# One super-step of a fused attention and MLP kernel, its order of loads, splits, merges and inversions written anew

## Chip, cores and metric

The kernel runs on one core of a Trainium2 chip. The metric is the device time of one execution in microseconds (us). Five engines matter here: PE (TensorE, with its weight loads shown as PEld), DVE (VectorE), ACT (ScalarE), POOL (GpSimd) and SP (SyncE), whose queue starts nearly all DMA transfers. Each engine works through its own instructions in order.

## What is computed

A delta-rule attention over 768 steps for 4 batches of 8 heads (head dimension 48) gives 3072 tokens of width 384, and two MLPs follow.

```python
for t in range(S):
    y[:, :, t] = einsum('bhd,bhde->bhe', q[:, :, t], state)
    v_old = einsum('bhde,bhd->bhe', state, kt)
    state = state + bt * einsum('bhd,bhe->bhde', kt, vt - v_old)   # kt: key / its norm
...
h = maximum(x @ w_in, 0.0); x = h * h @ w_out                      # d_ff 2048
g = x @ w_gate; out = silu(g) * (x @ w_val) @ w_out                # d_ff 1536
```

## The kernel before

**Tiles and stages.** The sequence is cut into six super-steps J of 128 steps, and each into two chunks c of 64 steps. A chunk's recurrence is solved with the inverse of a triangular 64x64 matrix per head: a Gram matrix of the keys (`gram`, `gram0`), its mask and scaling, the inverse of its 32x32 diagonal blocks, merges that join blocks (`m1`, `m2`), and then `ks` (old state times keys), `u`, `y` (output) and `ku` (state update). For J >= 1 the blocks go through DRAM: `mout` writes the matrices to `m_scr`, `tload` reads the diagonal blocks of all heads into the one tile `T`, `inv` eliminates 30 rows on POOL, `nout` writes `T` to `n_scr`, and `nback` and `mback` read them into `NT`. `t11` then transposes on DVE what `m1` multiplies. For J = 0 the diagonal blocks are inverted on DVE at once for both chunks (`inv0`, as 16x16 halves); `dout` transposes the result into the tiles `ND` and `NDT`, `d1` and `d2` are the merges of the halves (64 tiny matmuls a chunk each, counted twice in the trace since fp32 takes two passes), and `dcopy` copies the result.

**The first MLP** runs under the attention of the next super-step: 16 blocks m of 128 hidden units. `moe1_h` is x @ w_in of block m (one group of six matmul passes, lines 915 or 947), `moe1_o` its part of the output (line 989). In super-step 0 the first six blocks are done in two halves of 256 tokens. The weights come in 16 pieces (pc, kd) of 768 KB (kd 0: w_in, kd 1: w_out). Each is loaded by `load_w1`, decoded from 64-bit words by an ACT operation (line 157) and three DVE steps (lines 162, 164, 169; `conv`, and `ahead` for the ACT part alone), and later split into a high and a low part for the fast matmul format: `high` on ACT (line 184) and `low` on DVE (line 187). Super-step 0 multiplies by the decoded weights themselves, all but its last two blocks; from super-step 1 on the split parts are used. The pool of weight tiles is full, so a piece's split form takes the tile of the piece that was split before it. `split_x` splits the tokens of the next super-step.

**Order.** PE and SP follow the order of the program text. In super-step 0 so do DVE, ACT and POOL. Ahead of the first `moe1_h` stands a startup written out by hand. After it, `slot` is called twice for each block of the MLP, once after the next `moe1_h` and once after the `moe1_o`, and it adds to a clock: 0.5 for a half block and 1 for a whole one, so that super-step 0 has 32 units and whole block m has the slots 2m and 2m + 1. The table `first` says at which clock value a stage of the attention or a load is issued, `conv_slot` keeps decoding at 1.8 steps a unit, and `split_slot` splits pieces at a rate from a start value. The pieces that are not split when the last `moe1_h` of super-step 0 has been issued are split there, one behind the other:

```python
if J < NJ - 1 and nxt[0] == J and nxt[3] == NM1 - 1:
    if nxt[1] == 0:
        while split1:
            split_one()
        lows_out()
        split_x(J + 1, 0, HT)
```

At the end of super-step 0 the three accumulators are copied to two tiles `ye`, which a DMA on POOL's queue stores (line 1006); they share their buffers, so the second waits for the store of the first.

Of the kernel before, what the change touches and what calls it, by code (L numbers as in the profile page):

```python
# [21 lines left out]
def delta_attention_moe_moe2_kernel(  # L22
# [46 lines left out]
    TOK = 128 * B  # L69
    HT = TOK // 2  # L70
    HMS = [6, 2, 1, 1, 1, 1]
    LAGS = [0, 0, 4, 0, 0, 0]
    NC = S // 64

    const = ctx.enter_context(tc.tile_pool(name="const", bufs=1))
# [137 lines left out]
    def load_w1(pc, kd):  # L213
        if (pc, kd) == FIRST:
            raw = xp.tile([128, 2 * PIECE], I32, tag="xh", name="raw")
        else:
            raw = wp.tile([128, 2 * PIECE], I32, tag="w", name="raw")
        load_piece((w_in, w_out)[kd], pc, kd == 1, raw)
        loaded[pc, kd] = raw
# [253 lines left out]

    def d_out():
        nc.vector.transpose(out=ND.rearrange("s x t -> s t x"), in_=T)
        nc.vector.transpose(out=NDT.rearrange("t x s -> t s x"), in_=TT)

    def d_rest():

# [632 lines left out]
    def conv(n):  # L1112

        conv_to(converted() + n)
# [7 lines left out]
    def merge16(w, c):  # L1122
        run_all((w, c, p) for p in P2)
# [20 lines left out]
    load_w1(0, 1)  # L1144
    run(("v", 0, 1))
    load_w1(1, 0)
    nc.gpsimd.memset(mask, 0.0)
    for b0 in (0, 64):
        nc.gpsimd.affine_select(
# [28 lines left out]
    run(("drest",))  # L1178
    run(("vn", 0, 0))
    run(("dout",))  # L1180
    merge16("d1", 0)
    run(("sq", 1, 1, 1))
    run(("root", 1, None, 0))
    run(("root", 1, None, 1))
    stage("mmask", 1, 0)
    stage("mmask", 1, 1)
    conv(1)
    merge16("d2", 0)
    ahead()
    run(("t11", 0, 0))  # L1190
    run(("dcopy", 0))
    stage("mbeta", 1, 0)
    stage("mout", 1, 0)
    run(("m1", 0, 0))
    conv(2)
    ahead()
    run(("m2", 0, 0))
    stage("mbeta", 1, 1)
    stage("mout", 1, 1)
# [2 lines left out]
    conv(2)  # L1202
    run(("u", 0, 0))
    held.clear()
    conv(1)
    ahead()
    stage("y", 0, 0)
    run_all(("tload", 1, c) for c in P2)
    run(("v", 1, 0))
    run(("mback", 1, 0))  # L1210
    run(("ku", 0, 0))
    merge16("d1", 1)
    run(("vn", 0, 1))
    run(("inv", 1, 0, 1, nc.gpsimd))
    conv(3)
    load_w1(1, 1)
    load_w1(2, 0)
    run(("loadq", 1, 0))
    load_w1(2, 1)
    run(("loadk", 2, 0))  # L1220
    PRE = converted()
    startup.clear()

# [10 lines left out]
    if True:  # L1234

        LOW2 = 300
        CR = 0.6
        RATE = 0.8
        SPLIT0 = 14
        SPLIT = 0.7  # L1240
        seq = []
        for J in range(NJ):
            seq += [(J, c0, HT, m) for c0 in (0, HT) for m in range(HMS[J])]
            seq += [(J, 0, TOK, m) for m in range(HMS[J], NM1)]
        first = {
            0: [("d2", 1, 0), ("d2", 1, 1)],
            0.5: [("ks", 0, 1)],
            1: [("t11", 0, 1), ("m1", 0, 1), ("dcopy", 1)],
            2: [("m2", 0, 1), ("loadw", 3, 0)],
            3: [("u", 0, 1)],  # L1250
            4: [("y", 0, 1, 0), ("y", 0, 1, 1), ("loadw", 3, 1), ("loadq", 1, 1)],
            5: [("ku", 0, 1), ("loadk", 2, 1), ("mback", 1, 1), ("v", 1, 1)],
            6.5: [("loadw", 4, 0)],
            7: [("amm", 1, 0), ("acopy", 0)],
            8: [("sq", 2, 0, 0), ("loadw", 4, 1)],
            9: [("sq", 2, 0, 1), ("sq", 2, 1, 0)],
            9.5: [("loadw", 5, 0)],
            10: [("sq", 2, 1, 1), ("root", 2, None, 0)],
            11: [("root", 2, None, 1), ("loadw", 5, 1)],
            12: [("amm", 1, 1), ("acopy", 1)],  # L1260
            12.5: [("loadw", 6, 0)],
            13: [("gram", 2, 0)],
            14: [("loadw", 6, 1)],
            15: [("gram", 2, 1)],
            15.5: [("loadw", 7, 0)],
            16: [("vn", 1, 0), ("asel", 0), ("vn", 1, 1), ("asel", 1)],
            16.5: [("nout", 1), ("nback", 1, 0), ("tload", 2, 0), ("tload", 2, 1), ("nback", 1, 1)],
            17: [("inv", 2, 0, 1, nc.gpsimd)],
            17.5: [("loadw", 7, 1)],
            18: [("ks", 1, 0), ("t11", 1, 0)],  # L1270
            19: [("m1", 1, 0)],
            20: [("m2", 1, 0)],
            21: [("u", 1, 0), ("v", 2, 0), ("mback", 2, 0)],
            22: [("t11", 1, 1), ("y", 1, 0, 0), ("y", 1, 0, 1), ("loadq", 2, 0)],
            23: [("ku", 1, 0), ("loadk", 3, 0), ("fetch", 1, 0, HT)],
            24: [("m1", 1, 1)],
            25: [("ks", 1, 1)],
            26: [("m2", 1, 1)],
            28: [("u", 1, 1), ("v", 2, 1), ("mback", 2, 1), ("vn", 2, 0)],
            29: [("y", 1, 1, 0), ("y", 1, 1, 1), ("loadq", 2, 1)],  # L1280
            30: [("ku", 1, 1), ("fetch", 1, HT, HT), ("loadk", 3, 1)],
            31: [("nout", 2), ("nback", 2, 0), ("vn", 2, 1)],
            34: [("agram", 2, 0)],
        }
        timed = [(i, name) for i, names in first.items() for name in names]
        for C in range(2, NJ):
            lag = LAGS[C]
            timed += [(2 * NM1 * (C - 1) + lag + i - 3, s) for i, slot_ in enumerate(plan(C, C + 1)) for s in slot_]
        timed.sort(key=lambda s: s[0])
        clock = [0.0]  # L1290

        def slot(J, n_, m):
            while timed and timed[0][0] <= clock[0] + 1e-6:
                run(timed.pop(0)[1])
            clock[0] += n_ / TOK
            if J == 0:
                conv_slot(PRE + int(STEPS * CR * clock[0]))
            if J == 0:
                split_slot(J, m, SPLIT * (clock[0] - SPLIT0))

        def split_slot(J, m, n):
            lows_out()
            if split1 and NCONV - len(split1) < n and 2 * split1[0][0] + 1 < m:
                split_one()

        moe1_h(*seq[0])
        moe1_low()
        for n, it in enumerate(seq):
            J, c0, n_, m = it
            if n and J and not seq[n - 1][0]:  # L1310
                order.close()
                order.enter_context(tc.manual_schedule(engines={mybir.EngineType.DVE, mybir.EngineType.Activation}))
            nxt = seq[n + 1] if n + 1 < len(seq) else None
            if nxt:
                moe1_h(*nxt)
                if J and nxt == (J, 0, HT, HMS[J] - 1):
                    split_x(J, HT, HT)
# [6 lines that stand above are left out]
                    if nxt[1] + nxt[2] == TOK and HMS[J + 1] < 2:  # L1324
                        split_x(J + 1, HT, HT)
            else:
                moe2_g(0, 0, pool2)
            slot(J, n_, m)
            moe1_low()
            moe1_o(*it, pool2)  # L1330
            slot(J, n_, m)
            if n + 1 < len(seq) and J == NJ - 1 and pool2 is None and not xraw and not timed:
                order.close()
                att.__exit__(None, None, None)
                held.append(1)
                pool2 = ctx.enter_context(tc.tile_pool(name="p2", bufs=4))
                conv2 = [(pc, kd) for pc in range(NM2 // 2) for kd in range(3)]
                raws2 = [(pc, kd) for pc in range(NM2 // 2) for kd in range(3)]
                n_end = n
                for _ in range(3):  # L1340
                    load_w2(*raws2.pop(0), pool2)
            if J == NJ - 1 and m == NM1 - 4:
                load_x2(0, pool2)
            if J == NJ - 1 and m == NM1 - 2:
                split_x2(0)
            if pool2 is not None:

# [73 lines left out]
```

## Time and profile before

| | us |
|---|---|
| median of 3 runs | 1094.08 |
| lowest, highest of the runs | 1094.03, 1294.63 |
| profiled execution, device time | 1093.18 |
| its span (first to last instruction) | 1091.5 |
| PE busy | 1011.7 (93%) |
| DVE, ACT, POOL busy | 575.3, 402.7, 232.4 |

The profiled execution agrees with the median to 0.1%. Its device time is 1.7 us longer than its span. A busy PE is not yet a fast PE: the granted clock has two levels, 1.0 (2.4 GHz) and 0.5 (1.2 GHz), and a stretch's mean lies between them.

### The profile page before, as it was taken

Reading aid. Unit: us, or ns where it says so; the run is one execution under the profiler, and the core shown is the slowest. Engines: PE = TensorE matmul, PEld = TensorE weight load, DVE = VectorE, ACT = ScalarE, POOL = GpSimd, SP = SyncE. Lnnn points to the kernel's source line nnn. Section 1 sums busy time; section 2 is a strip of 40 time slices with the busy share of each in tenths; the row PEclk is TensorE's granted clock in tenths of the full one; section 3 lists DMA queues with packets and bytes.
Section 4 is the critical chain, followed back from the end, with each engine's and each line's share of the span. In section 5 each row is a group of like instructions: output and inputs, shape, how many; then the busy total and the mean of one; then the engine's idle time right before and its main releaser. Section 6 shows DMA issues by size and latency. Waiting matters only on the chain.

```text
span 1091.5 us, 24143 instructions
## 1 busy us (share of the span) xinstructions
PE 1011.7 (93%) x10454; PEld 812.7 (74%) x10454; DVE 575.3 (53%) x940; ACT 402.7 (37%) x756; POOL 232.4 (21%) x365
## 2 busy tenths in 40 slices
PE   4368989579999999999999999999999999999998
PEld 4357635467777788788787878888888888888886
DVE  7627674447767757645536996343343343433333
ACT  7324644424344344333336874222222222222222
POOL 3584229210860850770000000000000000000000
PEclk9979988789999999999999999999999999999999
DMA  9272463143353352331114661010010010100000
GB/s 274 57 215 69 165 164 96 40 123 64 97 153 77 88 132 70 83 96 38 31 30 155 194 223 66 1 58 1 1 58 1 25 34 1 59 1 0 29 1 29
DMA packets 118249, 84.49 MB, mean 77 GB/s; under 512 B 91648, under 2 KB 95616, under 8 KB 118144
## 3 DMA queue, kind: packets, MB, share of 16 engines
q1 hardware_dynamic: 116944, 77.97, 25.8%
q0 software_dynamic: 1056, 4.72, 1.1%
q8 instruction: 82, 1.34, 0.5%
q10 hardware_dynamic: 144, 0.26, 0.1%
q14 instruction: 23, 0.19, 0.1%
HBM read 61.70 MB, written 21.23 MB: 76 GB/s over the span
## 4 chain that ended last, share of the span: by engine, by line
PE 73%; issue 10%; DVE 7%; DMA 5%; ACT 4%; SPq 1%; POOL 0%; DVEq 0%; ACTq 0%; POOLq 0%
PE ps_o L1084 13%; PE ps_g L1059 13%; PE ps_v L1059 13%; PE ps_y L989 12%; PE ps_h L947 10%; PE ps_h L915 3%; DMA y_scr<-ye 1%; PE ps_y L753 1%; DMA raw<-in_moe_w_gate_dram 1%; PE ps_g L401 1%; PE ps_u L716 1%; DVE w L187 1%; PE ps_k L701 1%; PE ps_a L525 1%; PE ps_s L737 1%
## 5 line engine op out<-in xcount | busy, mean ns | idle before, releaser
L947 PE MATMUL ps_h<-xh,w 128*128 128x512 f32 (+1 forms) x540 | 170.6, 376 | 0.0
L989 PE MATMUL ps_y<-hh,w 128*128 128x512 f32 (+1 forms) x528 | 133.3, 387 | 15.9 <-ACT ye L1005 6.9
L1059 PE MATMUL ps_g<-x2h,w 128*128 128x512 f32 x432 | 144.8, 389 | 0.0
L1059 PE MATMUL ps_v<-x2h,w 128*128 128x512 f32 x432 | 144.7, 389 | 0.0
L1063 DVE SCALAR_TENSOR_TENSOR th<-th,ps_g 128x512 f32<-128x512 f32 x72 | 49.5, 688 | 170.8 <-ACT th L1062 170.7
L574 POOL TENSOR_TENSOR TMP<-T 128x30 f32<-128x30 f32 (+9 forms) x150 | 89.3, 595 | 157.3 <-DMA T<-m_scr 145.9
L989 PEld LDWEIGHTS ps_y<-hh,w 128*128 128x128 f32 x528 | 94.2, 191 | 34.6 <-ACT ye L1005 7.1
L950 ACT ACTIVATE r<-ps_h 128x512 f32<-128x512 f32 (+1 forms) x90 | 49.4, 549 | 181.6 <-PE ps_h L947 181.6
L947 PEld LDWEIGHTS ps_h<-xh,w 128*128 128x128 f32 x540 | 99.8, 191 | 18.1
L1084 PE MATMUL ps_o<-ph,w 128*128 128x512 f32 x432 | 111.9, 389 | 1.5 <-ACT ye L1005 1.5
L1062 ACT ACTIVATE th<-ps_g 128x512 f32<-128x512 f32 x72 | 43.0, 598 | 180.0 <-PE ps_g L1059 179.9
L947 PE MATMUL ps_h<-xl,w 128*128 128x512 f32 (+1 forms) x270 | 99.7, 369 | 0.0
L1084 PEld LDWEIGHTS ps_o<-ph,w 128*128 128x128 f32 x432 | 81.0, 188 | 18.7 <-ACT ye L1005 1.9
L1066 ACT ACTIVATE ph<-th 128x512 fp32r<-128x512 f32 x72 | 45.5, 632 | 133.2 <-DVE th L1064 133.2
L1059 PEld LDWEIGHTS ps_g<-x2h,w 128*128 128x128 f32 x432 | 81.1, 188 | 17.2 <-ACT hh L951 0.4
L1059 PEld LDWEIGHTS ps_v<-x2h,w 128*128 128x128 f32 x432 | 81.1, 188 | 16.9
L581 POOL TENSOR_TENSOR T<-T,TMP 128x30 f32<-128x30 f32 (+9 forms) x150 | 91.2, 608 | 11.3
L1059 PE MATMUL ps_g<-x2l,w 128*128 128x512 f32 x216 | 84.0, 389 | 0.0
L1059 PE MATMUL ps_v<-x2l,w 128*128 128x512 f32 x216 | 84.0, 389 | 0.0
L966 DVE TENSOR_TENSOR r<-r 128x512 f32<-128x512 f32 (+1 forms) x73 | 49.2, 675 | 64.1 <-ACT hh L951 63.8
L989 PE MATMUL ps_y<-hl,w 128*128 128x512 f32 (+1 forms) x264 | 72.0, 382 | 3.5 <-DVE hl L967 3.5
L1064 DVE SCALAR_TENSOR_TENSOR th<-th,ps_v 128x512 f32<-128x512 f32 x72 | 49.5, 688 | 44.8 <-PE ps_v L1059 44.7
(139 smaller groups left out, 1495.5 us busy)
## 6 DMA issues: line engine op xcount, KB each, us to landing
raw<-in_moe_w_out_dram SPq DMA_DIRECT2D x14, 768.0 KB, 5.4
raw<-in_moe_w_in_dram SPq DMA_DIRECT2D x8, 768.0 KB, 10.3
KT<-in_kt_dram SPq DMA_DIRECT2D x12, 448.0 KB, 5.3
m_scr<-M SPq DMA_DIRECT2D x20, 256.0 KB, 2.5
KB<-in_kn_dram SPq DMA_DIRECT2D x12, 384.0 KB, 5.2
AQ<-in_q_dram SPq DMA_DIRECT2D x24, 192.0 KB, 4.2
V<-in_v_dram SPq DMA_DIRECT2D x12, 384.0 KB, 3.7
raw<-in_moe_w_gate_dram SPq DMA_DIRECT2D x6, 768.0 KB, 4.4
```

The source lines that it names most:

```text
L574: eng.tensor_tensor(tmp[:, r0:r1], t_[:, r0:r1, kk:kk + 1].to_broadcast([n, r1 - r0, w]), t_[:, kk:kk + 1, kk + 1:].to_broadcast([n, r1 - ...
L581: eng.tensor_tensor(t_[:, r0:r1, kk + 1:], t_[:, r0:r1, kk + 1:], tmp[:, r0:r1], op=ALU.add)
L947: nc.tensor.matmul(ps, w_[:, kk], x_[:, kk, cols], start=n == 0, stop=n == 3 * KD - 1)
L950: nc.scalar.activation(out=r, in_=ps, func=ACTF.Relu)
L966: nc.vector.tensor_tensor(r, r, r, op=ALU.mult)
L989: nc.tensor.matmul(acc[f], w_[:, fs], h_, start=first, stop=m == NM1 - 1 and n == len(terms) - 1)
L1059: nc.tensor.matmul(ps, w_[:, kk], x_[:, kk], start=n == 0, stop=n == 3 * KD - 1)
L1062: nc.scalar.activation(out=th, in_=gp, func=ACTF.Tanh, scale=0.5)
L1063: nc.vector.scalar_tensor_tensor(out=th, in0=th, scalar=1.0, in1=gp, op0=ALU.add, op1=ALU.mult)
L1064: nc.vector.scalar_tensor_tensor(out=th, in0=th, scalar=0.5, in1=vp, op0=ALU.mult, op1=ALU.mult)
L1066: nc.scalar.activation(out=hh, in_=th, func=ACTF.Copy)
L1084: nc.tensor.matmul(o_acc[J][f], w_[:, fs], h_, start=m == 0 and n == 0, stop=m == NM2 - 1 and n == 2)
```

## The change

It touches startup and super-step 0 only, but for one number of a later plan. The weight pieces (1,1) and (2,0) are loaded before the startup's work; (2,1), the query and the key loads move from the end of the startup into the table. `dout` transposes only the half of `NDT` that `d1` reads. The square root of the norms is issued ahead of `d1` of chunk 0, a copy on POOL that reads the finished scale `bB` is put in front of the masks, and the three decoding steps of the first piece run ahead of `d2`. `d1` of chunk 1 moves behind the first `moe1_h`. In the table most stages from clock 6 on come 0.5 to 3.5 units sooner (`nout(1)` from 16.5 to 13.5, behind it now `tload` ahead of `nback`; `inv` of super-step 2 from 17 to 14), and all weights are loaded by clock 12. Splitting starts at 12 in place of 14, at 0.9 pieces a unit in place of 0.7, and under an exact condition on when a piece was last used. `LAGS[2]` goes from 4 to 3, which issues the attention of the next super-step one unit sooner.

```diff
-    LAGS = [0, 0, 4, 0, 0, 0]
+    LAGS = [0, 0, 3, 0, 0, 0]
...
-        nc.vector.transpose(out=NDT.rearrange("t x s -> t s x"), in_=TT)
+        nc.vector.transpose(out=NDT.rearrange("t x s -> t s x")[:, 0:16], in_=TT[:, 0:16])
...
     load_w1(1, 0)
+    load_w1(1, 1)
+    load_w1(2, 0)
...
     run(("dout",))
-    merge16("d1", 0)
     run(("sq", 1, 1, 1))
     run(("root", 1, None, 0))
+    merge16("d1", 0)
     run(("root", 1, None, 1))
+    nc.gpsimd.tensor_copy(mark, bB[:, 2, 0, 0:1])
     stage("mmask", 1, 0)
     stage("mmask", 1, 1)
-    conv(1)
+    conv(3)
     merge16("d2", 0)
-    ahead()
     run(("t11", 0, 0))
     run(("dcopy", 0))
+    ahead()
     stage("mbeta", 1, 0)
     stage("mout", 1, 0)
     run(("m1", 0, 0))
-    conv(2)
-    ahead()
+    conv(1)
     run(("m2", 0, 0))
     stage("mbeta", 1, 1)
...
     held.clear()
-    conv(1)
     ahead()
...
     run(("ku", 0, 0))
-    merge16("d1", 1)
...
     conv(3)
-    load_w1(1, 1)
-    load_w1(2, 0)
-    run(("loadq", 1, 0))
-    load_w1(2, 1)
-    run(("loadk", 2, 0))
     PRE = converted()
...
-        SPLIT0 = 14
-        SPLIT = 0.7
+        SPLIT0 = 12
+        SPLIT = 0.9
...
-            0.5: [("ks", 0, 1)],
-            1: [("t11", 0, 1), ("m1", 0, 1), ("dcopy", 1)],
+            0.5: [("ks", 0, 1), ("loadw", 2, 1)],
+            1: [("t11", 0, 1), ("m1", 0, 1), ("dcopy", 1), ("loadq", 1, 0)],
+            1.5: [("loadk", 2, 0)],
...
-            12: [("amm", 1, 1), ("acopy", 1)],
...
-            13: [("gram", 2, 0)],
-            14: [("loadw", 6, 1)],
-            15: [("gram", 2, 1)],
-            15.5: [("loadw", 7, 0)],
-            16: [("vn", 1, 0), ("asel", 0), ("vn", 1, 1), ("asel", 1)],
-            16.5: [("nout", 1), ("nback", 1, 0), ("tload", 2, 0), ("tload", 2, 1), ("nback", 1, 1)],
-            17: [("inv", 2, 0, 1, nc.gpsimd)],
-            17.5: [("loadw", 7, 1)],
-            18: [("ks", 1, 0), ("t11", 1, 0)],
-            19: [("m1", 1, 0)],
+            9: [("sq", 2, 1, 1), ("root", 2, None, 0), ("amm", 1, 1), ("acopy", 1)],
...
+            10.5: [("gram", 2, 0)],
+            11: [("loadw", 6, 1)],
+            11.5: [("loadw", 7, 0)],
+            12: [("gram", 2, 1), ("loadw", 7, 1)],
+            13: [("vn", 1, 0), ("asel", 0), ("vn", 1, 1), ("asel", 1)],
+            13.5: [("nout", 1), ("tload", 2, 0), ("tload", 2, 1), ("nback", 1, 0), ("nback", 1, 1)],
+            14: [("inv", 2, 0, 1, nc.gpsimd)],
+            16: [("ks", 1, 0)],
+            17: [("t11", 1, 0)],
+            18: [("m1", 1, 0)],
...
-            28: [("u", 1, 1), ("v", 2, 1), ("mback", 2, 1), ("vn", 2, 0)],
-            29: [("y", 1, 1, 0), ("y", 1, 1, 1), ("loadq", 2, 1)],
-            30: [("ku", 1, 1), ("fetch", 1, HT, HT), ("loadk", 3, 1)],
-            31: [("nout", 2), ("nback", 2, 0), ("vn", 2, 1)],
+            26.5: [("u", 1, 1), ("v", 2, 1), ("mback", 2, 1), ("vn", 2, 0)],
+            27.5: [("y", 1, 1, 0), ("y", 1, 1, 1), ("loadq", 2, 1)],
+            28.5: [("ku", 1, 1), ("fetch", 1, HT, HT), ("loadk", 3, 1)],
+            30: [("nout", 2), ("nback", 2, 0), ("vn", 2, 1)],
...
-            if split1 and NCONV - len(split1) < n and 2 * split1[0][0] + 1 < m:
-                split_one()
+            if split1 and NCONV - len(split1) < n:
+                pc, kd = split1[0]
+                if 2 * pc + 1 <= (m if kd else hm) or (split1[0] == LAST and not conv1 and not making):
+                    split_one()
 
         moe1_h(*seq[0])
+        merge16("d1", 1)
         moe1_low()
```

## Rows read from the trace of the kernel before

**Rows 1.** The page's 40 equal slices of 27.3 us: busy tenths, granted clock.
```profile
PE   4368989579999999999999999999999999999998
...
PEclk9979988789999999999999999999999999999999
```
**Rows 2.** Stretches: length, busy us (instructions) of each engine, PEclk, DMA share, GB/s.
```profile
60.50:75.90 15.40, 7.95 (x277) 6.49 (x269) 0.00 (x0) 4.44 (x11) 13.52 (x25) 0.67 0.93 287
130.00:148.70 18.70, 18.69 (x196) 9.19 (x187) 17.34 (x24) 9.79 (x14) 0.92 (x1) 1.00 0.64 170
148.70:174.20 25.50, 20.07 (x275) 10.89 (x275) 13.50 (x20) 8.45 (x17) 15.47 (x26) 0.73 0.47 94
194.00:220.90 26.90, 15.69 (x230) 13.18 (x229) 14.53 (x22) 10.79 (x18) 5.17 (x10) 0.75 0.27 64
220.90:234.00 13.10, 6.20 (x86) 5.90 (x86) 2.64 (x8) 3.17 (x8) 2.77 (x3) 0.61 0.71 206
340.00:1091.50 751.50, 741.99 (x5665) 609.66 (x5665) 369.62 (x559) 253.06 (x433) 83.84 (x136) 1.00 0.20 57
```
**Rows 3.** Timeline of PE: start, length, what; in brackets the idle before.
```profile
34.30 0.67 PE L637 MATMUL ps_d<-NDT,ND 16*32 16x16 f32 x35 [2.02 <-issue]
...
67.75 0.73 PE L637 MATMUL ps_d<-NDT,ND 16*32 16x16 f32 x41 [6.33 <-issue]
...
75.28 0.63 PE L655 MATMUL ps_e<-ND,NDT 32*32 32x16 f32 x53 [1.11 <-issue]
...
135.74 1.16 PE L401 MATMUL ps_g<-KT 48*64 48x64 f32 x64
136.83 2.85 PE L915 MATMUL ps_h<-x,raw 128*128 128x512 f32 x6
```
**Rows 4.** Timeline of DVE, startup and the stretch around 130 us.
```profile
28.77 1.93 DVE L476 STREAM_TRANSPOSE NDT<-T 128x1024 f32<-128x1024 f32 x1
...
37.76 1.17 DVE L360 TENSOR_TENSOR NS<-NS 128x32 f32<-128x32 f32 x1
...
47.09 1.28 DVE L457 TENSOR_TENSOR M<-M,bB 128x512 f32<-128x512 f32 x2
...
54.39 2.31 DVE L722 TENSOR_TENSOR RS<-ps_u,bB 64x384 f32<-64x384 f32 x4 [4.55 <-PE ps_u L716]
...
58.34 0.96 DVE L164 SCALAR_TENSOR_TENSOR raw<-raw,f 128x768 int32<-128x768 int32 x1
...
120.27 0.19 DVE L360 TENSOR_TENSOR NS<-NS 128x32 f32<-128x32 f32 x1
...
151.09 0.77 DVE L666 STREAM_TRANSPOSE tq<-NT 128x256 f32<-128x256 f32 x2 [1.71 <-DMA NT<-n_scr]
```
**Rows 5.** Timeline of POOL: masks, selects, steps of the two inversions.
```profile
30.45 4.92 POOL L453 TENSOR_TENSOR M<-M,mask 128x512 f32<-128x512 f32 x4
35.33 4.77 POOL L557 TENSOR_SCALAR_AFFINE_SELECT AQ<-AQ 64x1024 f32<-64x1024 f32 x4
...
56.99 0.90 POOL L581 TENSOR_TENSOR T<-T,TMP 128x58 f32<-128x58 f32 x1
...
156.77 0.25 POOL L574 TENSOR_TENSOR TMP<-T 128x30 f32<-128x30 f32 x1 [25.85 <-DMA T<-m_scr]
...
198.17 0.16 POOL L583 MEMSET T<- 128x32 f32 x1
```
**Rows 6.** Timeline of ACT: the last piece's decoding and a split of the burst.
```profile
160.73 0.91 ACT L157 ACTIVATE f<-raw 128x768 f32<-128x768 f32 x1 [6.13 <-DMA raw<-in_moe_w_out_dram]
...
197.85 0.89 ACT L184 ACTIVATE w<-raw 128x768 fp32r<-128x768 f32 x1 [1.06 <-DVE w L187]
```
**Rows 7.** Timeline of SP's queue around the return of the inverse.
```profile
142.06 0.34 SPq L608 DMA_DIRECT2D n_scr<-T  x1
147.84 1.92 SPq L623 DMA_DIRECT2D NT<-n_scr  x4
149.80 2.95 SPq L516 DMA_DIRECT2D T<-m_scr  x4
```

More of the change, by code (lines that the diff above doesn't have):

```diff
@@ L1246, in delta_attention_moe_moe2_kernel @@
             0: [("d2", 1, 0), ("d2", 1, 1)],
-            0.5: [("ks", 0, 1)],
-            1: [("t11", 0, 1), ("m1", 0, 1), ("dcopy", 1)],
+            0.5: [("ks", 0, 1), ("loadw", 2, 1)],
+            1: [("t11", 0, 1), ("m1", 0, 1), ("dcopy", 1), ("loadq", 1, 0)],
+            1.5: [("loadk", 2, 0)],
             2: [("m2", 0, 1), ("loadw", 3, 0)],
             3: [("u", 0, 1)],
-            4: [("y", 0, 1, 0), ("y", 0, 1, 1), ("loadw", 3, 1), ("loadq", 1, 1)],
+            3.5: [("loadw", 3, 1)],
@@ L1252, in delta_attention_moe_moe2_kernel @@
+            4: [("y", 0, 1, 0), ("y", 0, 1, 1), ("loadq", 1, 1)],
             5: [("ku", 0, 1), ("loadk", 2, 1), ("mback", 1, 1), ("v", 1, 1)],
[L1253 to L1259, printed above, removed]
-            12: [("amm", 1, 1), ("acopy", 1)],
@@ L1261, in delta_attention_moe_moe2_kernel @@
-            12.5: [("loadw", 6, 0)],
-            13: [("gram", 2, 0)],
-            14: [("loadw", 6, 1)],
-            15: [("gram", 2, 1)],
-            15.5: [("loadw", 7, 0)],
-            16: [("vn", 1, 0), ("asel", 0), ("vn", 1, 1), ("asel", 1)],
-            16.5: [("nout", 1), ("nback", 1, 0), ("tload", 2, 0), ("tload", 2, 1), ("nback", 1, 1)],
-            17: [("inv", 2, 0, 1, nc.gpsimd)],
-            17.5: [("loadw", 7, 1)],
-            18: [("ks", 1, 0), ("t11", 1, 0)],
-            19: [("m1", 1, 0)],
@@ L1272, in delta_attention_moe_moe2_kernel @@
[L1272 to L1278, printed above, removed]
-            28: [("u", 1, 1), ("v", 2, 1), ("mback", 2, 1), ("vn", 2, 0)],
-            29: [("y", 1, 1, 0), ("y", 1, 1, 1), ("loadq", 2, 1)],
-            30: [("ku", 1, 1), ("fetch", 1, HT, HT), ("loadk", 3, 1)],
@@ L1282, in delta_attention_moe_moe2_kernel @@
-            31: [("nout", 2), ("nback", 2, 0), ("vn", 2, 1)],
-            34: [("agram", 2, 0)],
+            6: [("loadw", 4, 0)],
+            7: [("sq", 2, 0, 0), ("amm", 1, 0), ("acopy", 0)],
+            7.5: [("loadw", 4, 1)],
+            8: [("sq", 2, 0, 1), ("sq", 2, 1, 0)],
+            8.5: [("loadw", 5, 0)],
+            9: [("sq", 2, 1, 1), ("root", 2, None, 0), ("amm", 1, 1), ("acopy", 1)],
+            9.5: [("loadw", 5, 1), ("root", 2, None, 1)],
+            10: [("loadw", 6, 0)],
@@ new lines, in delta_attention_moe_moe2_kernel @@
+            10.5: [("gram", 2, 0)],
[8 more added lines that the diff above has]
+            18: [("m1", 1, 0)],
+            19: [("m2", 1, 0)],
@@ new lines, in delta_attention_moe_moe2_kernel @@
+            20: [("u", 1, 0), ("v", 2, 0), ("mback", 2, 0)],
+            21: [("t11", 1, 1), ("y", 1, 0, 0), ("y", 1, 0, 1), ("loadq", 2, 0)],
+            22: [("ku", 1, 0), ("loadk", 3, 0), ("fetch", 1, 0, HT)],
+            23: [("m1", 1, 1)],
+            24: [("ks", 1, 1)],
+            25: [("m2", 1, 1)],
+            26.5: [("u", 1, 1), ("v", 2, 1), ("mback", 2, 1), ("vn", 2, 0)],
+            27.5: [("y", 1, 1, 0), ("y", 1, 1, 1), ("loadq", 2, 1)],
+            28.5: [("ku", 1, 1), ("fetch", 1, HT, HT), ("loadk", 3, 1)],
@@ L1284, in delta_attention_moe_moe2_kernel @@
+            30: [("nout", 2), ("nback", 2, 0), ("vn", 2, 1)],
+            32: [("agram", 2, 0)],
         }
@@ L1290, in delta_attention_moe_moe2_kernel, with slot @@
         clock = [0.0]
-        def slot(J, n_, m):
+        def slot(J, n_, m, hm=-1):
             while timed and timed[0][0] <= clock[0] + 1e-6:
@@ L1298, in slot, with split_slot @@
             if J == 0:
-                split_slot(J, m, SPLIT * (clock[0] - SPLIT0))
-        def split_slot(J, m, n):
+                split_slot(m, hm, SPLIT * (clock[0] - SPLIT0))
+        def split_slot(m, hm, n):
             lows_out()
-            if split1 and NCONV - len(split1) < n and 2 * split1[0][0] + 1 < m:
-                split_one()
+            if split1 and NCONV - len(split1) < n:
+                pc, kd = split1[0]
+                if 2 * pc + 1 <= (m if kd else hm) or (split1[0] == LAST and not conv1 and not making):
+                    split_one()
         moe1_h(*seq[0])
+        merge16("d1", 1)
         moe1_low()
@@ L1327, in delta_attention_moe_moe2_kernel @@
                 moe2_g(0, 0, pool2)
-            slot(J, n_, m)
+            whole = n_ == TOK
+            slot(J, n_, m - 1 if whole else -1, m + 1 if whole else -1)
             moe1_low()
             moe1_o(*it, pool2)
-            slot(J, n_, m)
+            slot(J, n_, m if whole else -1, m + 1 if whole else -1)
             if n + 1 < len(seq) and J == NJ - 1 and pool2 is None and not xraw and not timed:
```

## Prediction

> **What bounds the kernel now.** I first read the page's slices: PE is busy 9 tenths or more nearly everywhere from the tenth slice on, and what it leaves open lies in the first nine, some 245 us, where the granted clock drops too [rows 1]. From 340 us on PE is busy 742.0 of 751.5 us at clock 1.00 [rows 2], so nothing that the change does there can pay. Then I read stretches of super-step 0. The time that PE loses in one is its idle time plus its busy time times (1 - clock). That is 10.9 us in 148.7 to 174.2 (25.5 - 20.07 idle, 20.07 x 0.27 slow), 15.1 us in 194 to 220.9 (11.2 and 3.9), 9.3 us in 220.9 to 234 (6.9 and 2.4), and 10.1 us in 60.5 to 75.9 (7.45 and 2.6), where the startup ends [rows 2]. Last I read each engine's timeline there, for what came last at each gap [rows 3 to 7]. I take the four places one by one.
>
> **The end of super-step 0 (194 to 220.9).** By rate the old table has split 10 of 16 pieces when the last `moe1_h` is issued (0.7 x 14 units at clock 28), and 6 follow in a burst. In it ACT's high part waits for DVE's low part of the piece before, since it takes that piece's tile: 0.89 us of ACT after a wait of 1.06 on DVE [rows 6], about 1.95 us a piece, 11.7 for six. `moe1_o` of block 14 needs the third of them. The new rate gives 0.9 x 16 = 14.4 at clock 28, so 15 pieces are begun; I followed the new condition piece by piece, and it holds back none of them (piece (7,1) goes at 26, after all decoding). One is left. Besides, `u(1,1)` now comes ahead of the burst, so the scaled result that `y(1,1)` waits for no longer queues behind it on DVE. What is late next is the chain relu and squares, split of the last piece, `split_x`, some 5 us of ACT and DVE; `y`, `moe1_o` and `ku` on PE cover about 5 (estimates). Of 15.1 us I let 1 remain: gain 14. If that cover fails by 5 us, with the half clock behind it, 9; the upper end is 16.
>
> **The store behind it (220.9 to 234).** The second `ye` still waits for the store of the first, and the order there is the same. Only `ks(2,0)`, one unit sooner through `LAGS`, falls into this wait: gain 1 (its own length; 0 to 2). The store is queued on POOL behind the third inversion's end (156.77 to 198.17, 41.4 us [rows 5]). That inversion starts some 38 us ahead of the last `moe1_h` before and after, so it ends about 4 us behind it, two scalings of V of 1.5 us follow, and the store is due about 10 us behind it: 3 us of cover, and each us beyond it would lengthen the wait.
>
> **The middle (148.7 to 174.2).** Two waits: DVE's transposition at 151.09 waits for `nback` [rows 4], and ACT stands 6.13 us at the last piece's decoding, whose weights come late, with the copy that `u` needs behind it [rows 6]. The second goes: (7,1) is loaded at clock 12, ahead of `nout` on SP, and is not decoded before clock 18. For the first I count from the Gram matrix at 135.74 [rows 3]. `nout` follows 6.3 us after it, its landing lets `nback` go at +12.1, and the transposition starts at +15.35, although `m1` is due at 148.7, +13.0: one Gram matrix of 1.16, four blocks and `ks` of 1.1, so 2.69 a block [rows 2 to 4, 7]. Afterwards six blocks lie between: m1 is due at +18.4. But `tload` now stands ahead of `nback` on SP, and it overwrites `T`, so it too waits until `nout` has read it: 2.95 us are added [rows 7], and `nback` then shares the DMA engines with it. With 2 to 3.5 us for its issue and 1.3 to land, the transposed tile is there at 12.1 + 2.95 + 1.9 to 3.5 + 1.3 + 0.77 = +19.0 to +20.6. A wait of 0.6 to 2.2 us remains, and if the clock falls behind it, some 3 more. I let 3 of 10.9 us remain: gain 8 (3 to 11).
>
> **DVE's load there.** In 130 to 148.7 DVE is busy 17.34 of 18.7 us while PE loses nothing [rows 2]. From clock 12 to 22 it now has, per unit, 1.8 decoding steps (two of three cost 0.96 [rows 4], 2.5 us a piece, so 1.5), 0.9 low parts of 0.96 and about 1.05 of attention: 3.4 us, against 2.69 + 0.7 for PE. It just keeps up: cost 1, bounds 0 and 6.
>
> **The startup (to 75.9).** Norms: one small DVE operation takes 1.17 us while POOL selects and 0.19 when POOL is idle [rows 4]; five of the eight were held like this, about 4 us. The copy that waits for `bB` holds POOL's masks back until they are done, and the square root no longer queues behind `d1`, whose last stall ends at 34.30 [rows 3]. Half of the 1.93 us transposition goes too [rows 4]. So the norms end near 33 instead of 42. Behind the waiting copy stand POOL's four masks (4.92) and four selects (4.77) [rows 5], with a scaling of 1.5: 11.2 us that now run from 33.5 beside DVE's decoding of two pieces (5.0), four scalings of M (0.64 each [rows 4]) and two copies (0.9): 8.5 us. The first result `RS`, at 54.39 [rows 4], waited for `u` on PE, whose inputs ACT delivered late because the second piece's decoding stood ahead of them; `ahead` now stands behind. PE's chain alone would give RS at about 46.5. If DVE and POOL take strict turns, DVE comes to it at 33.5 + 11.2 + 8.5 = 53.2. The rows at 37.76 and at 56.99 (a POOL step of 0.90 where its neighbours of that size take 0.3) speak for turns [rows 4, 5], so I take a gain of 3 between 1.2 and 7.9. The Trainium skill, SBUF — State Buffer, section Who interferes with whom, states this as a rule that speaks against the change: VectorE with two SBUF inputs and GpSimd reading SBUF exclude each other for a whole instruction. By it the gain here is 1.2, and the sum 1067.
>
> Then `d1` of chunk 1. PE stood 6.33 us in the middle of it and again in `d2` at 75.28, 7.5 us later, waiting for nothing that the profile shows, each time after 128 more pairs of instructions, with the DMA engines 93% busy; at 34.30, with them idle, the same stall was 2.02 [rows 2, 3]. I read these as PE's instructions being fetched through busy DMA engines. Now the first `moe1_h` lies between, and two pieces (1.5 MB) are out of this queue: 0 to 5 gained, 2 taken. The two pieces are loaded in the startup instead, where they keep the queues busy until about 32; should the stall at 34.30 grow to 6.33, `d1` would be 4.3 late, which DVE's queue hides as long as it is the bound. The Trainium skill, Runtime: NRT & Kernel Launch, section Instruction fetch mechanics, says that a block's fetch is mostly hidden; these rows differ. If the stall were something else and stayed, the sum would be 1067. The masks, and so `mout`, `tload` and the second inversion, come between 2.4 us sooner and 3 us later; nothing waits for it before `nout` at clock 13.5, which hides either, and the cost without that cover is those 3 us. The loads on SP behind `mout` keep over 10 us to spare. Startup: gain 5, bounds 1 and 13.
>
> **Sum.** 14 + 1 + 8 + 5 - 1 = 27 us. From the profiled execution's 1093.2 us (0.9 below the median of 1094.1) that is 1066.
>
> **Rivals.** *Turns and transfers (19%).* DVE and POOL take strict turns and fetches stay as long (startup 1), `tload` ahead of `nback` leaves a wait of 4 us and a half clock (middle 3), and DVE's queue costs the end some (10): 14 gained, 1079. For it: the rows named; against it: six blocks instead of four, and no other piece in ACT's way. *All waits go (11%).* The ends of the first three gains, 16 + 11 + 12 + 1: 1053. Against it the added 2.95. *The change does not do what it says (6%).* If (7,1) is not decoded in time at clock 26, four pieces stay in the burst, 7.8 us in place of 2; with the half clock the end gains 6 only: 1074. *Slower (4%).* The denser splitting starves PE. ACT and DVE hand each piece to and fro at 1.95 us [rows 6]; if DVE falls a whole unit behind, each of 14 pieces makes ACT, and the relu behind it, late by that: 27 us, and at half clock in between as much again, against 27 gained: 1093.2 - 27 + 27 + 20 = 1113. It decides where DVE's work in a unit exceeds PE's 3.4 by more than 2 us; 3.4 against 3.4 speaks against it. The forecast has 60%.
>
> **Numbers.** The forecast's own bounds, with one term at its bad end and the others as taken, are 1055 to 1074, and the likelier half of the first rival takes the range to 1081; below, 1053. A measurement of this kernel tells about 2%, 22 us, from no change, so faster means under 1072. Nearly all of the forecast and the second rival lie there (0.68); the rest of the forecast, the first and the third rival lie within 2% (0.28); slower has 0.04.
>
> **What would show it.** In the profile of the changed kernel there should be one split behind the last `moe1_h`, and no PE gap of over 2 us between it and `moe1_h` of the next super-step; no ACT wait on a weight load; a wait of 1 to 2 us at the transposition ahead of `m1(1,0)`; small norm operations of 0.19 us, and then decoding steps and masks longer than before; RS between 47 and 53; a stall under 5 us in `d1` of chunk 1; the wait for `ye` unchanged. The prediction is wrong if DVE is busy without a gap from clock 12 to 22 and PE waits for it, or if the third inversion's end holds back the store.

## Result and profile after

| | us |
|---|---|
| median of 4 runs after | 1067.57 (1065.53 to 1070.16) |
| median of 4 runs of before beside them | 1094.05 |
| ratio after to before, 95% interval | 0.9768 [0.9736, 0.9800] |
| profiled execution after, and its span | 1070.16, 1068.5 |

The change takes 26.5 us off the median, and the forecast was 27. One run of before lies far above the others (1294.63) and is left out of the ratio. The profiled execution after is the slowest of its four runs and 23.0 us below that of before; a second profile of the same kernel (run f1 below) has a span of 1065.4, 26.1 less than before. I place the 23.0 first and come to the 3.1 between the profiles later.

The page's slices after, to be held against [rows 1]: the first nine are fuller, and one low clock is left among slices seven to nine where there were three.

```profile
PE   4569989799999999999999999999999999999998
...
PEclk9989989899999999999999999999999999999999
```

Stretches of the kernel after (columns as in [rows 2]):

```profile
60.50:75.90 15.40, 10.63 (x256) 8.37 (x257) 0.86 (x2) 2.51 (x6) 13.59 (x24) 0.67 0.57 166
...
141.00:163.00 22.00, 18.31 (x272) 10.09 (x274) 16.22 (x21) 11.73 (x20) 19.26 (x27) 0.77 0.27 44
163.00:186.00 23.00, 23.00 (x371) 11.94 (x366) 12.60 (x18) 12.13 (x21) 20.65 (x31) 1.00 0.37 95
186.00:212.00 26.00, 19.25 (x317) 16.85 (x316) 16.20 (x28) 9.60 (x20) 6.56 (x9) 0.80 0.54 153
212.00:235.00 23.00, 23.00 (x355) 19.07 (x355) 13.82 (x30) 11.18 (x25) 0.00 (x0) 1.00 0.15 28
...
340.00:1068.00 728.00, 718.47 (x5216) 590.82 (x5214) 351.18 (x531) 246.72 (x423) 76.56 (x123) 1.00 0.18 54
```

Idle plus slow time of PE, reckoned as in the prediction: 141 to 163 loses 7.9 us (3.69 idle, 18.31 x 0.23 slow), where before's middle lost 10.9. 186 to 212 loses 10.6, and behind it PE has no gap; before, the end of super-step 0 and the store behind it lost 15.1 and 9.3.

The timeline of PE after:

```profile
62.84 0.83 PE L637 MATMUL ps_d<-NDT,ND 16*32 16x16 f32 x47 [4.03 <-issue]
...
70.13 0.63 PE L655 MATMUL ps_e<-ND,NDT 32*32 32x16 f32 x53 [2.43 <-issue]
...
73.24 1.68 PE L701 MATMUL ps_k<-RS,KT 48*64 48x48 f32 x64
...
122.61 1.16 PE L401 MATMUL ps_g<-KT 48*64 48x64 f32 x64
...
143.56 1.39 PE L673 MATMUL ps_m<-tq,NT 32*32 32x32 f32 x64 [2.84 <-DVE tq L666]
...
154.55 2.54 PE L716 MATMUL ps_u<-V,NT 64*64 64x48 f32 x64 [0.88 <-issue]
...
182.97 1.15 PE L716 MATMUL ps_u<-V,NT 64*64 64x48 f32 x64
...
193.92 1.52 PE L737 MATMUL ps_s<-RS,KB 64*48 64x48 f32 x60 [2.52 <-ACT ys L760]
...
206.14 1.95 PE L701 MATMUL ps_k<-RS,KT 48*64 48x48 f32 x60 [4.23 <-DVE AQ L544]
```

Four of these rows serve as marks: `ks(0,1)` at 73.24 (78.37 before) ends the startup; the second Gram matrix at 122.61; `u(1,1)` at 182.97; `ks(2,0)` at 206.14. The startup gained 5.1. The last `moe1_h` ends at 186.8 instead of 193.98, though `u(1,1)` (1.15 us) now lies ahead of it: 8.3 gained up to there, so 3.2 in the middle. From there to the end of the last `moe1_o` (199.66) it is 12.8 us; before it was 25.76, with `u` inside: without it 11.8 gained. The rest of the 23.0, 2.9, comes behind that. No PE wait for `ye` is left; `ks(2,0)` waits 4.23 us for DVE instead. What it waits for stands at the end of a longer chain, by ACT's and DVE's timelines: ACT waits for the attention's output to come back from DRAM (`xr`), makes the high part of the tokens' second half, DVE makes the low part (`xl`), and then come the second `ye` and `AQ`.

```profile
202.69 1.03 ACT L819 ACTIVATE xh<-xr 128x256 fp32r<-128x256 f32 x3 [1.10 <-DMA xr<-xs_scr]
...
203.14 1.09 DVE L820 TENSOR_TENSOR xl<-xr,xh 128x256 fp32r<-128x256 f32 x3 [3.25 <-ACT xh L819]
204.27 0.42 DVE L1003 COPY ye<-ps_y 128x256 f32<-128x256 f32 x1
204.61 2.80 DVE L544 TENSOR_TENSOR AQ<-ps_a,mask 64x512 f32<-64x512 f32 x4
```

The timeline of DVE after, startup and middle: the first norm step is short again, and what runs beside POOL is long.

```profile
31.46 0.19 DVE L360 TENSOR_TENSOR NS<-NS 128x32 f32<-128x32 f32 x1
...
33.21 2.04 DVE L164 SCALAR_TENSOR_TENSOR raw<-raw,f 128x768 int32<-128x768 int32 x1
...
41.15 3.05 DVE L457 TENSOR_TENSOR M<-M,bB 128x512 f32<-128x512 f32 x2
...
49.88 2.31 DVE L722 TENSOR_TENSOR RS<-ps_u,bB 64x384 f32<-64x384 f32 x4
...
142.97 0.77 DVE L666 STREAM_TRANSPOSE tq<-NT 128x256 f32<-128x256 f32 x2 [2.53 <-DMA NT<-n_scr]
```

POOL after: the waiting copy, masks and selects (4.92 and 4.77 in [rows 5]), the end of the third inversion, the two scalings of V behind it, and the store of `ye`, which waits for its data and not for POOL.

```profile
32.84 0.38 POOL L1187 COPY mark<-bB 128x1 f32<-128x1 f32 x1 [2.69 <-DVE bB L364]
33.18 6.37 POOL L453 TENSOR_TENSOR M<-M,mask 128x512 f32<-128x512 f32 x4
39.50 5.70 POOL L557 TENSOR_SCALAR_AFFINE_SELECT AQ<-AQ 64x1024 f32<-64x1024 f32 x4
...
187.80 0.16 POOL L583 MEMSET T<- 128x32 f32 x1
187.88 3.63 POOL L300 TENSOR_TENSOR V<-V,nB 128x768 f32<-128x768 f32 x2
200.49 0.74 POOL L1006 DMA_DIRECT2D y_scr<-ye  x1 [8.98 <-DVE ye L1003]
```

SP's queue around the return of the inverse, against [rows 7]:

```profile
128.21 1.51 SPq L136 DMA_DIRECT2D raw<-in_moe_w_out_dram  x1
129.83 0.40 SPq L608 DMA_DIRECT2D n_scr<-T  x1
135.80 2.37 SPq L516 DMA_DIRECT2D T<-m_scr  x4
138.22 4.45 SPq L623 DMA_DIRECT2D NT<-n_scr  x8
```

ACT's waits from 110 to 215 us (us in total, times, longest). None is for a weight load any more (7.5 before, 6.1 of it for the last piece), but the high parts now wait 24.9 us for DVE's low parts, 11.2 before.

```profile
ACT w L184 <- DVE w L187: 24.9, 9, 5.7
```

### The profile page after: what moved, and what is told of

It reads as the page before. It is cut to its first block, busy times and chain, and to the rows that moved or that the text cites. A ratio compares the mean times of both kernels' runs of the same rounds, so it can differ in the third digit from the quotient of the medians.

```text
span 1068.5 us, 24149 instructions
## 1 busy us (share of the span) xinstructions
PE 1006.3 (94%) x10454; PEld 809.5 (76%) x10454; DVE 582.2 (54%) x940; ACT 401.9 (38%) x756; POOL 239.4 (22%) x366
## 4 chain that ended last, share of the span: by engine, by line
PE 64%; issue 9%; DMA 3%; DVE 3%; ACT 2%; POOL 0%; SPq 0%; ACTq 0%; DVEq 0%; POOLq 0%
PE ps_o L1084 14%; PE ps_v L1059 13%; PE ps_g L1059 13%; PE ps_y L989 9%; PE ps_h L947 9%; PE ps_y L753 1%; DMA y_scr<-ye 1%; DMA raw<-in_moe_w_gate_dram 1%; PE ps_k L701 1%; DVE raw L164 1%; DMA x2raw<-y_scr 1%; PE ps_g L401 1%; PE ps_a L525 1%; ACT f L157 1%; PE ps_u L716 1%
## 5 line engine op out<-in xcount | busy, mean ns | idle before, releaser
L581 POOL TENSOR_TENSOR T<-T,TMP 128x30 f32<-128x30 f32 (+9 forms) x150 | 95.0, 634 | 11.3
```

What stands on the lines that cost most here:

```text
L581: eng.tensor_tensor(t_[:, r0:r1, kk + 1:], t_[:, r0:r1, kk + 1:], tmp[:, r0:r1], op=ALU.add)
```

## Experiments

Ratios are to the kernel before, run on the same chip; the kernel after stands at 0.9768 [0.9736, 0.9800] and, again as f1, at 0.9767 [0.9749, 0.9785].

### The four parts

**e1_old_split**: the kernel after with the old splitting.

```diff
-        SPLIT0 = 12
-        SPLIT = 0.9
+        SPLIT0 = 14
+        SPLIT = 0.7
...
-            if split1 and NCONV - len(split1) < n:
-                pc, kd = split1[0]
-                if 2 * pc + 1 <= (m if kd else hm) or (split1[0] == LAST and not conv1 and not making):
-                    split_one()
+            if split1 and NCONV - len(split1) < n and 2 * split1[0][0] + 1 < m:
+                split_one()
...
```

> The changed kernel with the old rate, start and condition of the splits; all else stays. If the shorter burst is what shortens the end of super-step 0, about five more pieces at 1.95 us stand behind the last moe1_h of super-step 0, with half clock behind them: 8 to 12 us more than the changed kernel's 1067.6, so 1075 to 1080. Rival: the end is shorter because u(1,1) and y(1,1) are issued ahead of the burst and the burst is hidden: at most 3 us more, 1071 or less.

1077.64 us, 0.9864 [0.9845, 0.9883]: about 10 us slower than the kernel after. PE's waits from 180 to 235 us in e1 show the burst again, now at three places:

```profile
PE ps_k L701 <- DVE AQ L544: 7.4, 1, 7.4
PE ps_s L737 <- ACT ys L760: 4.8, 1, 4.8
PE ps_y L989 <- ACT w L184: 4.6, 1, 4.6
```

**e2_split_only**: the kernel before with the new splitting alone (e1's edit the other way round).

> The kernel before with the new rate, start and condition of the splits alone. First theory: the burst's loss of 15 us goes by 8 to 11, since u(1,1) and y(1,1) are still behind it: 1083 to 1086 against 1094. Rival as above: the burst alone is worth at most 3, 1091 or more. If the denser splitting costs the middle, it shows here as a longer stretch between the two Gram matrices of super-step 2 and the last moe1_h.

1081.66, 0.9908 [0.9883, 0.9933]: 10.7 us gained. The splitting is worth some 10 us either way, alone or with the rest, and the rival in which it only moves the wait falls. Undone (e1) it also shortens the middle: from the second Gram matrix to `u(1,1)` e1 takes 54.8 us and f1 57.3. So the denser splitting costs 2.5 there (1.3 by e2, whose stretch takes 59.5 us and that of before 58.2), and its gain at the end is some 12. In e2 `moe1_o` no longer waits for a split, but the scaled result does, as before [rows 2, 6]; PE's waits from 140 to 240 us:

```profile
PE ps_y L753 <- DVE RS L722: 5.1, 1, 5.1
PE ps_y L989 <- ACT ye L1005: 4.2, 1, 4.2
```

Both are gone in the kernel after, where `u(1,1)` stands ahead of the last splits.

**e4_old_startup**: the kernel after with the old startup: the two early loads, the order of `d1`, `conv`, `ahead` and the square root, the copy on POOL, the full transposition and the clocks of (2,1) and of the two loads as before.

> The changed kernel with the whole startup of before: loads, norms, masks, decoding and merges in their old places; table and splits as changed. If the startup is worth what the first matmuls of the traces differ by, 5 us, the time is 1071 to 1075. Rival one: what comes sooner in the startup is waited for later, 1068 or less. Rival two: the startup carries most of the gain, 1080 or more.

1071.10, 0.9806 [0.9785, 0.9827]: the startup is worth about 4 us. In the profile `ks(0,1)` starts at 78.74 instead of 73.24.

### The middle: which step costs

**e3_nback_first**: only the order of two steps.

```diff
-            13.5: [("nout", 1), ("tload", 2, 0), ("tload", 2, 1), ("nback", 1, 0), ("nback", 1, 1)],
+            13.5: [("nout", 1), ("nback", 1, 0), ("tload", 2, 0), ("tload", 2, 1), ("nback", 1, 1)],
```

> The changed kernel with nback of chunk 0 issued ahead of tload again, as before the change. If tload ahead of it is what keeps PE waiting at m1(1,0), the transposed tile comes about 2.4 us sooner than the 20.4 us after the second Gram matrix that the changed kernel shows, m1 waits less than 0.5 us in place of 2.84, and with the half clock behind it 3 to 6 us go: 1062 to 1065. Rival: ACT's and DVE's exchange of split pieces bounds the middle, so that under 1 us goes: 1067. The price would be the third inversion 2 us later, with 9 us to spare.

1065.49, 0.9757 [0.9734, 0.9780]: 1 to 2 us faster by the medians, with intervals that overlap. PE's wait ahead of `m1` is gone, but 1.25 us come back at `ps_x`:

```profile
140.95 1.04 PE L673 MATMUL ps_m<-tq,NT 32*32 32x32 f32 x64 [0.22 <-DVE tq L666]
...
146.01 0.24 PE L688 MATMUL ps_x<-NT,tq 32*32 32x32 f32 x2 [1.25 <-ACT tq L660]
```

From the second Gram matrix to `u(1,1)` it is 55.6 us (f1 57.3). So the moved `tload` costs under 2 us, and something else takes more.

**g3_late_last**: the load of (7,1) alone goes back to clock 17.5.

```diff
-            12: [("gram", 2, 1), ("loadw", 7, 1)],
+            12: [("gram", 2, 1)],
...
+            17.5: [("loadw", 7, 1)],
```

> The changed kernel with only the load of the last piece (7,1) back at clock 17.5, behind nout, tload and nback on SP. If that load held ACT and with it u(1,0), ACT waits some 3 to 6 us for it again and the middle loses 3 to 7 us: 1070 to 1074. Rival: with nout three units sooner the load comes in time anyway, and less traffic stands ahead of nout: 1067 or less.

1060.78, 0.9703 [0.9685, 0.9721]: 7 us faster than the kernel after, and my theory falls: the rival holds. The timelines of SP and DVE in g3:

```profile
129.00 0.34 SPq L608 DMA_DIRECT2D n_scr<-T  x1
132.15 2.14 SPq L516 DMA_DIRECT2D T<-m_scr  x4
134.33 4.87 SPq L623 DMA_DIRECT2D NT<-n_scr  x8
...
140.69 0.76 DVE L666 STREAM_TRANSPOSE tq<-NT 128x256 f32<-128x256 f32 x2
```

`nout` lets `tload` go 3.15 us after its issue; with the 768 KB piece issued just ahead of it, after 5.97 (129.83 to 135.80 above). Whether the order of the queue or the shared DMA engines make the difference was not separated. Everything behind it is about 3 us sooner, the transposition no longer waits, and the stretch to `u(1,1)` takes 52.3 us, 5.0 less than f1. ACT does not wait for the late piece: it is issued at 143.99 and its decoding starts at 149.91 with no wait. In before it was issued at 17.5 too, but behind `nback`, which came 3 units later.

**g1_lows_first**: DVE's low part of a split piece, which stood behind the slot's attention steps on DVE's queue, is issued at the head of the next slot.

```diff
         def slot(J, n_, m, hm=-1):
+            if J == 0:
+                lows_out()
```

> The changed kernel with the pending low part issued on DVE at the head of a slot, ahead of that slot's attention and decoding, in place of behind them. If ACT's high part, waiting for DVE's low part behind the transposition, is what makes the copies of m1 and m2 late in the middle (waits of 5.1 and 2.1 us on ACT in the changed kernel), those waits go and 2 to 4 us with them: 1063 to 1065. Rival: DVE itself is the bound there, the attention's operations then stand behind the low part, and the time stays within 1 us or grows.

1063.42, 0.9726 [0.9707, 0.9746]: some 4 us faster, as expected. ACT's waits for low parts fall from 24.9 to 9.9 us, the stretch to `u(1,1)` to 55.4 us, and PE's wait for `ys` from 2.52 to 0.99. Its wait for `AQ` grows from 4.23 to 6.56: what that waits for, `xr` from DRAM, is no low part of a weight, and ACT now waits 3.4 us for it.

**h1_lows_and_late**: g1 and g3 together.

> The changed kernel with both single edits: the load of (7,1) back at clock 17.5, and DVE's low parts at the head of a slot. Theory: the two edits remove different costs (the first the wait of the transposition ahead of m1(1,0), 2 to 3 us with the clock behind it and an ACT wait at its piece; the second the hand-off of each piece between DVE and ACT, 15 us of ACT's waiting spread over the super-step), so their gains of about 7 and 4 us over the changed kernel add up to at least half of the smaller one on top of the larger: 1056 to 1059 us, a ratio to before of 0.967 to 0.969; ACT waits on DVE's low part under 12 us between 110 and 215 us, no wait at m1(1,0). Rival: both gains are the same slack on ACT, so that together they give no more than the larger alone: 1060 to 1061, a ratio of 0.970 or more.

1058.95 (1057.97 to 1061.85 in 5 runs), 0.9694 [0.9681, 0.9707]: the fastest kernel of the study, 33.5 us below before, but between the two theories: beside g3's 0.9703 its interval doesn't settle whether the two gains add. In its profile they do up to `ks(2,0)`: there is no wait at `m1`, the stretch to `u(1,1)` is down to 51.1 us, ACT waits for a low part once, and `ks(2,0)` starts 3.4 us sooner than in g3 (199.16). The two lines are from ACT's waits (110 to 215 us) and PE's timeline:

```profile
ACT w L184 <- DVE w L187: 1.7, 1, 1.7
```

```profile
195.76 1.95 PE L701 MATMUL ps_k<-RS,KT 48*64 48x48 f32 x60 [5.14 <-DVE AQ L544]
```

From `ks(2,0)` to its end this profile takes 864.4 us, g3 860.4, and the kernel after 862.4; that part is the same code in all three, and the profiled execution of h1 is the slowest of its five. Of the 4.0 us more than in g3, 2.8 are PE's waits for DVE's `hl` (4.4 us, 1.6 in g3; the kernel after has 3.2 and its repeat f1 2.6), which differ between profiles of the same code; the rest is not explained.

### The startup and the rest

**f1_after_again**: the kernel after, unchanged, for the spread of its places.

> The changed kernel once more, as the measure for the runs beside it and for how much of a term of 2 us one profiled execution can show: 1065 to 1070, and the places of its waits as in the first profile.

1067.17, span 1065.4. `ks(0,1)` at 73.29 (73.24), the second Gram matrix at 123.53 (122.61), `u(1,1)` at 180.81 (182.97): the 3.1 us between the two profiles lie in the middle, where the stretch takes 57.3 us in place of 60.4. In e4 and f4, whose middle is the same, it takes 57.2 and 57.9; so the profile on record is the odd one, and the middle's gain is rather 5 to 6 than 3.2.

**f2_no_mark**: without the copy that holds POOL back.

```diff
-    nc.gpsimd.tensor_copy(mark, bB[:, 2, 0, 0:1])
```

> The changed kernel without the copy on POOL that waits for the finished scale: the masks run beside the norms again. If DVE and POOL take strict turns, only the place of the turns moves: the norms' five operations cost about 1.2 us each again, the decoding behind them meets selects in place of masks, and RS starts within 1.5 us of the changed kernel's 49.9; the time stays within 2 us. Rival: the copy saves the 4 us that the norms lose: RS at 53 to 55, the time 2 to 4 us longer.

1066.14, 0.9763 [0.9745, 0.9782]: no difference. The norms are long again, the decoding is shorter, and RS comes 0.3 us later. DVE's timeline in f2:

```profile
32.83 1.19 DVE L360 TENSOR_TENSOR NS<-NS 128x32 f32<-128x32 f32 x1
...
50.20 2.31 DVE L722 TENSOR_TENSOR RS<-ps_u,bB 64x384 f32<-64x384 f32 x4 [1.63 <-PE ps_u L716]
```

DVE and POOL hold each other up either way, and the copy only chooses which of DVE's steps bear it. Without it DVE is free for `RS` 1.3 us sooner (48.57), but `u` on PE starts at 47.25 instead of 43.24, and `RS` waits 1.63 us for it.

**f3_d1_back**: `d1` of chunk 1 ahead of the first `moe1_h` again.

> The changed kernel with d1 of chunk 1 back ahead of the first moe1_h. If its stall is a fetch of a fixed length that begins at the block before, the matmul group no longer covers a part of it: the stall grows from 4.0 to 5 to 6.5 us, and the merges of chunk 1 end 1 to 2.5 us later. Rival: the stall belongs to d1 itself, stays at 4, and nothing is lost.

1065.99, 0.9753 [0.9730, 0.9776]: not slower, so moving the merge is worth nothing. The stall in `d1` is 4.67 and that in `d2` shrinks to 0.39: a sum of 5.1, where the kernel after has 6.5 and its repeat f1 4.6. The ends of the two stalls stand 7.25 us apart (7.29 after, 7.01 in f1), and `ks(0,1)` starts at 73.21. A stall that shrinks by as much as the work put ahead of it is longer points to something of a fixed length running beside PE.

**f4_late_loads**: (1,1) and (2,0) loaded at the end of the startup again.

```diff
-    load_w1(1, 1)
-    load_w1(2, 0)
...
     conv(3)
+    load_w1(1, 1)
+    load_w1(2, 0)
```

> The changed kernel with the loads of pieces (1,1) and (2,0) at the end of the startup again. If busy DMA engines stretch the fetches, 1.5 MB more are in the queues at 55 to 62 us: the two stalls in d1 and d2 of chunk 1 grow from 6.5 us together to 8 or more, 1 to 4 us in all. Rival: a fetch is as long whatever else moves: no change there, and the early merges, freed of 1.5 MB at 28 to 32 us, not sooner either.

1070.52, 0.9798 [0.9780, 0.9817]: about 3 us slower, nearly all that the startup gives. PE's timeline in f4: both stalls are longer, with the DMA engines 86% busy from 60.5 to 75.9 us in place of 57%, and from one to the next it is 8.39 us instead of 7.29.

```profile
63.28 0.84 PE L637 MATMUL ps_d<-NDT,ND 16*32 16x16 f32 x47 [4.57 <-issue]
...
71.67 0.93 PE L655 MATMUL ps_e<-ND,NDT 32*32 32x16 f32 x53 [3.52 <-issue]
```

**g2_lag4**: `LAGS[2]` at 4 again.

> The changed kernel with LAGS[2] at 4 again. If moving ks(2,0) into the wait behind super-step 0 is worth its length, 1 us is lost: 1068 to 1069. Rival: the new wait there (ks for a PSUM bank that DVE's masking of the second Gram product of super-step 2 frees, 4.2 us) takes the place of the wait for ye and costs more, so that the old lag is 1 to 3 us faster: 1064 to 1066.

1067.01, 0.9754 [0.9739, 0.9768]: no difference. The wait of `ks(2,0)` for DVE's `AQ` is gone (`ks(2,0)` starts at 207.92 without one) and the wait for `ye` is back with 5.4 us, now not for the store but for DVE's copy, which stands behind `xl`; ACT waits 3.8 us for `xr` there.

## Why the prediction came out right

The total was right to 0.5 us of the change, and that is in part luck: its terms were not all so, and their errors cancel. In f1, whose span is 26.1 us below that of before, the end (11.2 of 14) and the middle (5.4 of 8 - 1) bring 4.4 us less than forecast, and what follows super-step 0 brings 3.4 more (4.4 of 1). Some side sums were off, without weight for the forecast: its terms, one at a time at their bad or good end, give 1058 to 1071 and not 1055 to 1074, and the two sums called 1067 are 1068.

- **End of super-step 0**, gain 14: right in mechanism, a little too large. 11.8 in the times; e1 and e2 give some 10 net. One split was left behind the last `moe1_h`, as said, but the cover I counted for the chain behind it was short: PE waits 2.52 us for `ys`, which stands on ACT behind the last piece's split and `split_x`, and 4.23 for `AQ`, which stands on DVE behind `xl`, and the granted clock there is 0.80 (186 to 212). That is the failing of cover for which the bound of 9 stood.
- **The store behind it**, gain 1: too small, 2.9. I said that the wait for `ye` would stay. It went: the second `ye` is held by `xl` and no longer by the store of the first, and `ks(2,0)`'s wait for `AQ` behind the same `xl` takes its place; g2 shows that the sooner `ks(2,0)` only exchanges the one wait for the other. POOL was done with the inversion and both scalings 9.0 us ahead of the store (191.51, 200.49), with more cover than the 3 us I had.
- **The middle**, gain 8: too large, 3.2 on record and some 5 to 6 with f1, the cost on DVE inside. The tile came 0.5 us behind the range: transposed at 143.74, 21.1 us behind the Gram matrix at 122.61, against 19.0 to 20.6, and `m1` waited 2.84 us against 0.6 to 2.2; in f1 it came at 20.0 and `m1` waited 1.73. The step that failed is "(7,1) is loaded at clock 12, ahead of `nout` on SP", which I booked as a gain alone. I counted every queue that `tload` passes but not the piece ahead of `nout`: g3 shows that it costs 3 us of `nout`'s landing, that the middle is 5.0 us shorter without it, and that ACT, for which it was moved, didn't need it.
- **DVE's load there**, cost 1, bounds 0 and 6: undersized but in its bounds; 2.5 by e1, 1.3 by e2. PE rarely waits for DVE directly. ACT does, 24.9 us, because a low part stands behind attention steps in DVE's queue, and ACT's own queue holds what PE needs. g1 and h1 take this wait away by order alone, at the same load.
- **The startup**, gain 5: right, 5.1 in the profile and 4 by e4, though put together differently. RS came at 49.88, 4.5 sooner than before instead of 3. DVE and POOL held each other up (L164 at 2.04 in place of 0.96, the masks at 6.37 in place of 4.92), but not in strict turns all the way: those would have put RS at 53.2. The copy, and the short norms, were worth nothing (f2). That a VectorE step with two SBUF inputs and a GpSimd step that reads SBUF exclude each other is what the Trainium skill, SBUF — State Buffer, section Who interferes with whom, says, and for L164 and the masks the trace agrees. What I gave to the merge moved behind `moe1_h` belongs to the two early loads (f3, f4).

Of the rivals, *turns and transfers* came near in two places: the end, for which it had 10 (11.8, and some 10 by e1 and e2), and the middle, for which it had 3 (3.2, and 5.4 in f1). It failed in the startup, which it put at 1: the turns were not strict and the stalls did shorten. The slower one failed at its condition: PE is busy for all of 163 to 186 us, while ACT waits.

That a PE stall without a releaser is its instructions arriving late can be read in the traces. The page's DMA queue of kind "instruction" moved 82 blocks of 16 KB, and PE ran 10454 pairs, 20908 instructions: 256 to a block, or 128 pairs.

```profile
q8 instruction: 82, 1.34, 0.6%
```

The 14 profiles have 72 such PE stalls of over 1 us, all in the first 77 us, and every one ends 1.2 to 1.9 us after a block has landed: in the kernel after, the blocks that land at 61.36 and 68.72 are followed by the starts at 62.84 and 70.13, and before, those at 66.33 and 73.73 by 67.75 and 75.28. The blocks take 0.9 to 1.7 us to move. What can be long is the time before the next one starts to move. In the kernel after it is 4.8 us behind the stall in `d1`, with the DMA engines full, and 1.15 us behind that in `d2`, with them idle (length, busy us of each engine, PEclk, DMA share, GB/s):

```profile
62.84:67.60 4.76, 4.76 (x128) 3.71 (x128) 0.00 (x0) 1.19 (x4) 4.21 (x8) 0.50 1.03 295
70.13:71.28 1.15, 1.15 (x55) 1.10 (x56) 0.00 (x0) 0.46 (x2) 1.04 (x2) 0.91 0.00 0
```

Thirteen profiles show the first stall, with 4.4 to 5.7 us behind it; f4, which only puts two loads back, has the longest. Twelve show 1.1 to 1.2 us behind the second. It is not the clock: f3 has 4.8 us at clock 1.00. That the full engines hold the block back fits all this but was not isolated: larger matmuls follow the first stall, and in f2 a block started 1.5 us behind a stall with the engines 98% busy. The Trainium skill, Runtime: NRT & Kernel Launch, section Instruction fetch mechanics, says that a block's fetch is mostly hidden; in the kernel after, 6.5 us of `d1` and `d2` are not.

## What to carry to other kernels

A load that is issued sooner also stands ahead of whatever follows it in its queue: look for the small transfer with a chain behind it that is issued next, and put the load behind that. Two engines that hand tiles to and fro can wait more for each other's queue order than for each other's work (24.9 and 9.9 us here, at the same work), so issue the hand-over first in a slot before cutting its rate. And when several edits go in at once, take each out alone: here the whole gained 26.5 us, the copy on POOL, the moved merge and the lag nothing, and one load cost 7.

## What the runs showed that was not expected

- The same 512 KB store `nout` let its reader go after 3.15 us with no piece on the way (g3) and after 5.97 behind a 768 KB piece issued 1.6 us ahead, in the same queue. In h1, where a piece issued 6.3 us ahead took 7.8 us to land, it was 4.29. In before, too, a piece stood 1.1 us ahead of it (140.93, 142.06), and it took 5.78 [rows 7].
- PE's stalls for the next 128 pairs end 3.45 us apart with the DMA engines nearly idle (33.35 and 36.80 us; 17% busy from 30 to 46) and 7.0 to 8.4 apart from 60.5 to 75.9 us, where they are 55 to 96% busy, whether 2.9 or 5.5 us of `moe1_h` lie between.
- Two engines in turns both pay: beside POOL's masks a decoding step of DVE takes 2.04 us in place of 0.96, and beside DVE the four masks take 6.37 in place of 4.92.
